# Dropping zero products from the set-up of a fused convolution and feed-forward kernel, moving set-up work between engines and between matmuls, and its last store to ScalarE

## The chip, the cores and the metric

The kernel runs on one core of a Trainium2 chip. The metric is the device time of one execution in microseconds (us), the lower the better. A core has five engines: TensorE (PE in the profile: matmuls), VectorE (DVE), ScalarE (ACT), GpSimd (POOL) and SyncE (SP, which mostly issues DMA transfers).

## The reference

```python
# x: 8 x 4160 x 192, weight: 8 heads x 7 taps
w = softmax(weight)                                  # over the 7 taps
y[b, s, h, :] = sum_k w[h, k] * x_pad[b, s + k, h, :]      # causal convolution, 24 channels a head
y = y.reshape(33280, 192)
h = maximum(maximum(y @ w1, y @ w2), y @ w3)         # 192 x 768 each
out = h @ w_out                                      # 768 x 192, fp32 out
```

## The kernel before

The 33280 tokens are cut into 65 blocks of 512. For each block TensorE does the convolution as matmuls with a banded matrix (`band`), then the "first layer" `l1(t, j)` for six tiles j of 128 hidden units, then the second layer with `w_out`.

The kernel saves a third of the first layer with a rearrangement: max(y·w1, y·w2, y·w3) = max(relu(y·(w1−w3)), y·(w2−w3)) + y·w3. So the set-up has to compute the differences `wd` (w1−w3 in 64 partitions, w2−w3 in the other 64) and the product m = w3·w_out, so that out = h·w_out + y·m. For m it first transposes w3 on TensorE.

```python
def keep_warm(n, pool=psw, tag="w"):      # n products of zeros, to raise TensorE's clock
    ps = pool.tile([P, NBLK], FP32, tag=tag, name="idle")
    for _ in range(n):
        nc.tensor.matmul(ps[:], lhsT=idle[:, 0:P], rhs=idle[:], start=True, stop=True)

def make_wd(j0, j1):                      # the differences for tiles j0 .. j1-1
    f = slice(P * j0, P * j1)
    nc.vector.tensor_sub(out=wd[:, :, f], in0=ws[:, :, f], in1=w3s[:, :, f])

def make_m(i):                            # a part of m = w3 . w_out
    ps = psp.tile([P, D], FP32, tag="p", name=f"pm{i}")
    ...                                   # 6 or 12 matmuls of w3t and wo
    nc.vector.tensor_copy(out=m16[:, i, :], in_=ps[:])

def cross(t, cs=range(NC)):               # second copy of y in the other 64 partitions: VectorE
    ...
def cross_dma(t):                         # the same by two transfers inside SBUF
    yd = dense[t]
    nc.sync.dma_start(out=yd[HALF:P, 0:NC:2, :], in_=yd[0:HALF, 0:NC:2, :])
    nc.sync.dma_start(out=yd[0:HALF, 1, :], in_=yd[HALF:P, 1, :])

def l1(t, j):
    ...                                   # lp and lq: 3 + 3 matmuls into two PSUM tiles
    nc.scalar.activation(out=r[:, 0:N], in_=ps[0][:, 0:N], func=AF.Relu)
    nc.vector.tensor_max(out=hs[t][:, j, 0:N], in0=r[:, 0:N], in1=ps[1][:, 0:N])
```

The order in which the set-up is written is the order on each engine:

```python
    conv_dense(0, (nc.scalar.copy, nc.scalar.copy, nc.scalar.copy))   # first convolution
    keep_warm(4)
    cross(0, (0,))
    make_wd(1, 2)
    cross(0, (1, 2))
    l1(0, 0)
    ...
    conv_dense(1, (nc.scalar.copy, nc.scalar.copy, nc.scalar.copy))   # second convolution
    keep_warm(4)
    cross(1)
    make_wd(2, 3)
    l1(1, 0)
    ...                                   # tiles of blocks 0 and 1 with the rest of the set-up
    l1(0, 5)
    cast_dense(2, (nc.gpsimd.tensor_copy, nc.gpsimd.tensor_copy))
    conv_dense(2, (nc.scalar.copy, nc.vector.tensor_copy, nc.scalar.copy))   # third convolution
    ...
    cross_dma(2)
    ...
    make_m(0)
    make_m(1)
    l1(1, 4)                              # "the next first layer" below
```

The softmax here doesn't subtract the row's maximum and nothing guards it: scores larger than these inputs give would overflow.

## Time and profile before

Three runs gave 479.44, 480.50 and 480.67 us, median 480.5. The profiled execution took 479.41 us; its span on the core is 477.6 us.

| | busy us | share of span |
|---|---|---|
| TensorE | 470.7 | 99% |
| VectorE | 365.7 | 77% |
| ScalarE | 325.6 | 68% |
| GpSimd | 213.2 | 45% |

TensorE sets the time. The main loop gives it work without a gap, two blocks in about 13.95 us, and the change leaves the loop alone. What can be won lies in the first 31 us and in the last 4. This is TensorE's own timeline of before, with its start and busy time in us, the line, what it computes, the shape and the count, and in brackets how long it had stood still and for whom:

```profile
4.97 3.59 PE L215 MATMUL idle<-idle 128*128 128x512 f16 x8
8.49 1.90 PE L318 MATMUL D<-band,xz 112*32 112x103 f16 x60
10.33 1.04 PE L215 MATMUL idle<-idle 128*128 128x512 f16 x4
...
24.44 1.09 PE L318 MATMUL D<-band,xz 112*32 112x103 f16 x60
26.89 0.37 PE L374 MATMUL lp<-yd,wd 64*128 64x512 f16 x1
```

The eight zero products take 3.59 us, the four later ones 1.04: the first ran at half clock (0.43 us apart), the later at full clock (0.22 apart). L318 is a convolution. The first starts at 8.49, the third at 24.44, and the next first layer follows it by 2.45 us.

### The profile page before, as it was taken

How to read it: one execution, taken by the hardware profiler on the slowest of the kernel's cores; microseconds unless marked ns; L12 is line 12 of the kernel's file. 1: busy time of each engine (PE TensorE's matmuls, PEld its weight loads, DVE VectorE, ACT ScalarE, POOL GpSimd, SP SyncE). 2: the span in 40 equal slices, each digit the busy share in tenths (PEclk: the TensorE clock that was granted, in tenths of full speed). 3: DMA queues.
4: the chain of work that ended last, by engine and by line, in shares of the span. 5: the costliest groups of instructions: out<-in, count | busy, mean ns of one | idle time of the engine just before them, and what ended most of it. 6: DMA issues, size and time to landing. Idle time of an engine off the chain costs nothing.

```text
span 477.6 us, 21859 instructions
## 1 busy us (share of the span) xinstructions
PE 470.7 (99%) x9042; PEld 392.3 (82%) x9042; DVE 365.7 (77%) x610; ACT 325.6 (68%) x610; POOL 213.2 (45%) x347
## 2 busy tenths in 40 slices
PE   8999999999999999999999999999999999999995
PEld 4478888888888888888788888888888888888995
DVE  4767778778777877877777787877778787777774
ACT  4757666676666767666676766667667666766664
POOL 3636543553454355255445534534553454455200
PEclk9999999999999999999999999999999999999999
DMA  8775866666765666657577667656676765764423
GB/s 191 166 198 151 238 186 175 179 180 162 197 192 159 175 172 185 169 162 201 152 193 183 181 164 205 177 152 190 171 183 166 201 180 153 190 172 107 107 76 100
DMA packets 68481, 81.68 MB, mean 171 GB/s; under 512 B 9342, under 2 KB 57470, under 8 KB 68382
## 3 DMA queue, kind: packets, MB, share of 16 engines
q1 hardware_dynamic: 55438, 49.51, 41.6%
q0 software_dynamic: 12928, 30.78, 21.2%
q8 instruction: 71, 1.16, 1.1%
q14 instruction: 28, 0.23, 0.2%
q10 hardware_dynamic: 16, 0.00, 0.0%
HBM read 30.31 MB, written 25.56 MB: 117 GB/s over the span
## 4 chain that ended last, share of the span: by engine, by line
PE 97%; DVE 1%; issue 0%; ACT 0%
PE lp L374 32%; PE po L418 30%; PE lq L374 26%; PE G L299 7%; PE idle L215 2%; PE D L318 1%; DVE h L379 0%; PE band_cols L237 0%; DVE yd L334 0%; DVE yd L325 0%; DVE w3s L258 0%; ACT yd L324 0%; DVE wd L254 0%; DVE m L284 0%; DVE o L428 0%
## 5 line engine op out<-in xcount | busy, mean ns | idle before, releaser
L379 DVE TENSOR_TENSOR h<-r,lq 128x512 f16<-128x512 f16 x390 | 267.2, 685 | 100.0 <-ACT r L378 98.6
L378 ACT ACTIVATE r<-lp 128x512 f16<-128x512 f32 x390 | 232.8, 597 | 138.6 <-PE lp L374 91.2
L374 PE MATMUL lp<-yd,wd 64*128 64x512 f16 x1170 | 315.6, 376 | 0.1
L374 PE MATMUL lq<-yd,wd 64*128 64x512 f16 x1170 | 314.7, 375 | 0.8 <-DVE h L379 0.6
L418 PE MATMUL po<-wo,h 64*128 64x192 f16 x3120 | 230.2, 243 | 0.0
L418 PEld LDWEIGHTS <-h 64*128 64x128 f16 x3120 | 186.2, 94 | 25.8
L374 PEld LDWEIGHTS <-wd 64*128 64x128 f16 x2340 | 163.9, 93 | 24.1 <-issue 4.2
L444 POOL DMA_DIRECT2D out_dram<-o x64 | 51.2, 799 | 237.0 <-DVE o L428 221.7
L357 POOL DMA_DIRECT2D yd<-ys x183 | 92.7, 512 | 1.8 <-ACT ys L344 1.0
L418 PE MATMUL po<-m,yd 64*128 64x192 f16 x780 | 86.9, 243 | 0.0
L428 DVE TENSOR_TENSOR o<-a,po 128x384 f32<-128x384 f32 (+1 forms) x132 | 71.4, 542 | 1.0 <-ACT a L427 1.0
L427 ACT COPY a<-po 128x384 f32<-128x384 f32 (+1 forms) x132 | 61.7, 468 | 1.8 <-PE po L418 1.8
L418 PEld LDWEIGHTS <-yd 64*128 64x128 f16 x780 | 54.7, 94 | 8.1
L151 POOL CAST x<-xf 112x960 f16<-112x960 f32 x60 | 59.6, 995 | 2.5 <-DMA xf<-in_x_dram 2.4
L344 DVE CAST ys<-G 128x512 f16<-128x512 f32 x61 | 39.2, 683 | 0.0
L299 PEld LDWEIGHTS <-x 112*32 112x32 f16 x2400 | 28.6, 96 | 12.7 <-issue 12.3
L344 ACT CAST ys<-G 128x512 f16<-128x512 f32 x61 | 32.9, 588 | 1.3
L299 PE MATMUL G<-band,x 112*32 112x103 f16 (+1 forms) x2400 | 33.3, 209 | 0.0
L215 PE MATMUL idle<-idle 128*128 128x512 f16 x24 | 9.2, 527 | 1.2 <-DVE idle L210 1.2
L170 POOL CAST xz<-xf 112x240 f16<-112x240 f32 (+2 forms) x15 | 4.9, 375 | 7.7 <-DMA xf<-in_x_dram 7.3
L215 PEld LDWEIGHTS <-idle 128*128 128x128 f16 x24 | 2.6, 122 | 5.5 <-issue 3.8
L318 PEld LDWEIGHTS <-xz 112*32 112x32 f16 x240 | 4.7, 107 | 2.5 <-DVE wd L254 0.8
(48 smaller groups left out, 47.2 us busy)
## 6 DMA issues: line engine op xcount, KB each, us to landing
xf<-in_x_dram SPq DMA_DIRECT2D x57, 420.0 KB, 4.5
out_dram<-o POOLq DMA_DIRECT2D x62, 384.0 KB, 4.2
yd<-yd SPq DMA_DIRECT2D x61, 192.0 KB, 3.7
yd<-ys SPq DMA_DIRECT2D x61, 48.0 KB, 3.8
yd<-ys POOLq DMA_DIRECT2D x61, 48.0 KB, 3.5
xf<-in_x_dram SPq DMA_DIRECT2D x8, 252.0 KB, 4.3
yd<-ys POOLq DMA_DIRECT2D x61, 32.0 KB, 3.5
yd<-ys SPq DMA_DIRECT2D x61, 32.0 KB, 3.4
```

The costliest lines, as they stand in the source:

```text
L151: nc.gpsimd.tensor_copy(out=v[0:rl, q0:q1, :], in_=xf[0:rl, q0:q1, :])
L215: nc.tensor.matmul(ps[:], lhsT=idle[:, 0:P], rhs=idle[:], start=True, stop=True)
L299: nc.tensor.matmul(G[i][32 * g:32 * g + 32, lo:hi], lhsT=x16[0:rlen, cb:cb + 32], rhs=band[0:rlen, h, cc:cc + hi - lo], start=True, stop=T ...
L344: copy(out=slots[t][:, i, :], in_=convs[t][i][:])
L357: (nc.sync, nc.gpsimd)[n % 2].dma_start(out=yd[r0:r0 + rows, c, :], in_=slots[t][s0:s0 + rows, half, :])
L374: nc.tensor.matmul(ps[i][:, 0:N], lhsT=wd[row, c, P * j:P * (j + 1)], rhs=y[row, c, 0:N], start=(c == 0), stop=(c == NC - 1))
L378: nc.scalar.activation(out=r[:, 0:N], in_=ps[0][:, 0:N], func=AF.Relu)
L379: nc.vector.tensor_max(out=hs[t][:, j, 0:N], in0=r[:, 0:N], in1=ps[1][:, 0:N])
L418: nc.tensor.matmul(ps[b0, i][:, s % 2, :], lhsT=a, rhs=b, start=first, stop=last)
L427: nc.scalar.copy(out=a[:, ss, :], in_=ps[s0, 0][:, ss, :])
L428: nc.vector.tensor_add(out=outs[t][:, s0:s + 1, :], in0=a[:, ss, :], in1=ps[s0, 1][:, ss, :])
L444: qs[0].dma_start(out=bass.AP(tensor=out.tensor, offset=r * D, ap=[[D, n], [step * D, s1 - s0], [1, D]]), in_=ob[p0:p0 + n, s0:s1, :])
```

## The change

The intent is to shorten the set-up and the end. Six zero products go. Three subtractions of 384 columns (128 in each of three parts) go from VectorE to GpSimd, the last two joined into one of 768, since VectorE's work stands ahead of work that TensorE waits for. The transposes and the first product of m are placed between other first layers, its copies go to ScalarE. The last of the final stores is issued by ScalarE, because SyncE is late with it. The core of the diff:

```diff
-    keep_warm(8, psp, "p")
+    keep_warm(5, psp, "p")
 ...
-    def make_wd(j0, j1):
+    def make_wd(j0, j1, eng=nc.vector):
 ...
-        nc.vector.tensor_copy(out=m16[:, i, :], in_=ps[:])
+        nc.scalar.copy(out=m16[:, i, :], in_=ps[:])
 ...
-                    store(t, s - (s == 1), s + 1, (nc.sync,))
+                    store(t, s - (s == 1), s + 1, (nc.scalar if s == 3 else nc.sync,))
 ...
-    make_wd(1, 2)
+    make_wd(1, 2, nc.gpsimd)
 ...
-    keep_warm(4)
+    keep_warm(3)
     cross(1)
 ...
     cast_w3(2)
-    keep_warm(1)
+    transpose_w3(1)
+    make_wd(4, 6, nc.gpsimd)
     l1(0, 3)
-    make_wd(4, 5)
-    transpose_w3(1)
+    transpose_w3(2)
     l1(1, 2)
-    make_wd(5, 6)
-    keep_warm(1)
     l1(1, 3)
-    transpose_w3(2)
     l1(0, 4)
     nc.gpsimd.tensor_copy(out=wo[:], in_=wos[:])
+    make_m(0)
     l1(0, 5)
 ...
-    make_m(0)
     make_m(1)
```

More of the change, by code (lines that the diff above doesn't have):

```diff
@@ L250 @@
     m16 = const.tile([P, 2, D], FP16)
-    def make_wd(j0, j1):
+    def make_wd(j0, j1, eng=nc.vector):
         f = slice(P * j0, P * j1)
-        nc.vector.tensor_sub(out=wd[:, :, f], in0=ws[:, :, f], in1=w3s[:, :, f])
+        eng.tensor_sub(out=wd[:, :, f], in0=ws[:, :, f], in1=w3s[:, :, f])
     def copy_w3(copy, part):
@@ L306, in conv, with conv_dense @@
         xin.pop(t)
-    def conv_dense(t, copies, pools=((psw, "w"), (psw, "w"))):
+    def conv_dense(t, copies):
         yd = dense[t] = ydp.tile([P, NC, NBLK], FP16, tag="yd", name=f"yd_{t}")
         for n, slots_ in enumerate((range(4), range(4, 6))):
-            ps = pools[n][0].tile([P, NBLK], FP32, tag=pools[n][1], name=f"D{n}_{t}")
+            ps = psw.tile([P, NBLK], FP32, tag="w", name=f"D{n}_{t}")
             for (q, b, row_lo, rlen, lo, hi, cc) in chunks_of[t]:
```

## The prediction

> **What bounds the kernel now.** I read the page first. Its busy line and its slices say where a change can pay:
>
> ```profile
> PE 470.7 (99%) x9042; PEld 392.3 (82%) x9042; DVE 365.7 (77%) x610; ACT 325.6 (68%) x610; POOL 213.2 (45%) x347
> PE   8999999999999999999999999999999999999995
> ```
>
> TensorE fills every slice but the first and the last (a slice is 477.6 / 40 = 11.9 us). The change touches neither the 63 blocks of the main loop nor their matmuls; it edits the set-up, which the timeline shows from 0 to about 31 us, and the last store. So its whole worth is idle and filler time in those two ends. The stretch view gives TensorE 15.59 us busy of the first 17 and 13.74 of the next 14.5, but part of that is products of zeros (24 of them, 9.2 us busy), so I went on to the chain of waits of the set-up:
>
> ```profile
> 13.58 0.69 DVE w3s L258
> 14.30 0.69 DVE h L379
> 15.02 0.91 DVE yd L334
> 15.97 0.37 PE lq L374
> ...
> 22.50 0.55 DVE wd L254
> 23.06 0.61 DVE h L379
> ...
> 25.75 0.69 DVE yd L325
> 26.48 0.37 DVE m L284
> 26.89 0.37 PE lp L374
> ```
>
> The set-up hangs on VectorE three times: around 14 us (copy of w3, a maximum, the copy yd that lets the second block's first layer start), at 22.5 (a subtraction ahead of a maximum that frees a PSUM buffer), and at 26.5 (m is copied out before the next first layer gets its PSUM buffer). Then GpSimd's own timeline, which shows what transfers dictate:
>
> ```profile
> 11.03 0.97 POOL L170 CAST xz<-xf 112x240 f16<-112x240 f32 x3 [7.33 <-DMA xf<-in_x_dram]
> ...
> 14.07 0.82 POOL L258 COPY w3s<-w3s 64x768 f32<-64x768 f32 x1 [0.54 <-DMA w3s<-in_moe_w_dram]
> 14.95 0.82 POOL L262 CAST w3h<-w3s 64x768 f16<-64x768 f32 x1
> 18.74 1.14 POOL L491 CAST wo<-wos 128x1152 f16<-128x1152 f32 x1 [2.97 <-DMA wos<-in_moe_w_out_dram]
> 20.27 3.96 POOL L170 CAST xz<-xf 112x240 f16<-112x240 f32 x12 [0.39 <-DVE h L379]
> ```
>
> The DMA engines are 0.94 busy over the first 17 us. The third block of x was issued at 13.57 and took 6.5 us, so it landed at 20.07: that, not the named maximum, is what the 12 casts at 20.27 waited for. The first six make block 2's input; SyncE issues the next load, which waits for them, at 22.26. So block 2's convolution, at 24.44 now, cannot run through before about 22.3 whatever the change does: 2.1 us is the ceiling of the set-up's gain.
>
> At the other end the last addition ends at 473.59, but SyncE is late with its last stores:
>
> ```profile
> 472.56 1.42 SPq L444 DMA_DIRECT2D out_dram<-o  x1
> 474.08 0.41 SPq L444 DMA_DIRECT2D out_dram<-o  x1
> 474.54 0.45 SPq L444 DMA_DIRECT2D out_dram<-o  x1
> ```
>
> The last store is issued 474.54 - 473.59 = 0.95 us after its data is ready, because an earlier issue took 1.42 us.
>
> **What the Trainium skill says.** "TensorE: Matmul & The Clock Gate", Part 1: the array starts at half clock and reaches full clock after a window of about 3.4 us of sustained work, at a phase that varies between runs. The trace agrees: idle matmuls of 512 columns last 0.63 us before 8.5 us and 0.39 at 10.33, and the first convolution's matmuls 0.29 against 0.21 later, so full clock came at about 10.3 us.
> "GPSIMD Engine Reference", 3.1: an fp32 two-input elementwise operation of 2048 columns takes 4497 ns on GpSimd. Scaled, an estimate from that page: 384 columns 0.84 us, 768 columns 1.69 us. The trace of before has no such operation on GpSimd; VectorE needs 0.556 for 384.
> "SBUF - State Buffer", "Who interferes with whom": a VectorE copy in a two-port mode and a GpSimd instruction exclude each other for the whole instruction. The trace agrees:
>
> ```profile
> 15.02 0.90 DVE L334 COPY yd<-yd 64x512 f16<-64x512 f16 x1
> ...
> 15.95 0.29 DVE L334 COPY yd<-yd 64x512 f16<-64x512 f16 x1
> ```
>
> The first copy ran into GpSimd's cast of 14.95 to 15.77. The same section lets VectorE's two-input operations contend with GpSimd's reads; here the subtractions at 21.44 and 22.50 ran beside the casts in an unchanged 0.55, so I charge those nothing.
> "DMA: Bandwidth & Descriptors", "Issuing engines are not separate DMA queues": a second issuing engine saves issue time only. That is just what the last store lacks.
>
> **The change part by part.**
> 1. *Three fewer zero products before the first convolution.* They run cold, 0.427 apart ((3.59 - 0.61) / 7), so the convolution starts 3 x 0.427 = 1.28 us earlier, at 7.2; its band is copied by 6.83, so it can. But full clock should still come near 10.3: the convolution then ends at 9.05, and of the four zero products that follow three run cold (1.28 us) instead of warm (0.65). The first layer of block 0 starts at about 10.5 instead of 11.30: **0.8 us** earlier.
> 2. *Subtraction 1 to GpSimd.* 0.56 us leave VectorE at 10.52. GpSimd is idle from 3.7 to 11.03 and the weights are there at 7.40; with 0.84 us (estimate) it is done by 8.4. Free, but the first layer it feeds did not wait for it: 0.
> 3. *Second convolution.* Block 1's x lands at 11.03, GpSimd's casts end at 12.0, ScalarE's, behind the relu of block 0, at 12.65 instead of 13.49. It keeps the 0.8 us. Copies of yd start at about 14.2 instead of 15.02.
> 4. *Here I take something back.* GpSimd's copy and cast of 14.07 to 15.77 stay where the weight transfer puts them, and the new 768-column subtraction follows at once, to about 17.5. VectorE's copy of w3 (now at 12.7) meets GpSimd's casts of 12.0 to 13.5, and the three yd copies meet the rest. Unhindered, the gain here is 0.8; with one instruction lost to the lock it is 0; with the long subtraction ahead of the last yd copy it is -1. I weigh these 0.5, 0.35, 0.15 and get 0.4 - 0.15 = **0.25 us**. A convolution at full clock earlier in some executions could add up to 0.4.
> 5. *First layers from 18.3 to 24.4.* Six in 6.15 us, 1.03 apart. With two PSUM buffers a pair needs relu 0.6, maximum 0.69, drain 0.37 and semaphores, about 2.0, so 1.0 each is the floor. Two subtractions (2 x 0.55) and two zero products (0.2 each) go, but only some 0.35 us of waits with them (0.33 and 0.2 to 0.35 at the last three). The product placed before the last first layer takes a turn of its PSUM pool, so that layer waits for a newer relu: -0.2. Net **0.15 us**.
> 6. *m on ScalarE, one product moved.* After the convolution the next first layer starts 24.44 to 26.89 = 2.45 us later; it becomes 1.03 + 0.62 = 1.65, 0.8 us less. But block 2's first layer, at 31.02, waits for the second yd transfer (issued 26.96, 4.0 us, landed 30.96), which hangs on the convolution, not on m. TensorE now gets there 0.15 us early; it will get there 0.95 early and wait. Worth **0**.
> 7. *Last store on ScalarE.* Issue at about 473.65 instead of 474.54, 0.9 us earlier; but the store before it is still issued at 474.08, and the 384 KB of the last three leave between 474.5 and 475.9 in nearly full engines. I count **0.35 us**.
> Sum: 0.25 + 0.15 + 0 + 0.35 = 0.75 us from these, and 0.2 for the chance of early full clock: 0.95.
>
> **Rivals.** *The lock on SBUF becomes the wait* (part 4): for it, the 0.90 copy above; against it, with the 0.8 shift one of the copies may slip in before 14.07. It alone would give about +1 us over my sum, 480.5. *All gains add up*: then the ceiling of block 2's casts binds, 2.1 us, and the store gives 0.5: 477.9. *The clock falls back to half* because zero products left: against it, gaps between matmuls stay near 1 us, far below a window; it would cost 2 to 3 us, 482. *The moved products feed through*: if the 0.8 of part 6 counts, 478.7.
>
> **Range and chances.** The three runs of before are 479.44 to 480.67, and the profiled one is among the fast (479.41), so the median itself carries some 0.6 us of luck. 480.5 - 0.95 = 479.55; before's mean of 480.2 would give 479.25; I say 479.4, with 478.2 to 480.6 for eight in ten. Two per cent is 9.6 us, beyond everything in the set-up that could be won or lost: within 2% at 0.98.
>
> **What would show it.** In the changed profile: the first convolution at 7.2 and the first layer of block 0 at 10.5 (part 1 right); a GpSimd subtraction of about 0.84 and one of 1.7 us; yd copies of VectorE longer than 0.29 beside it (part 4); block 2's convolution between 22.3 and 24.4, not waiting for its casts; block 2's first layer waiting for its yd transfer (part 6); the last store issued by ScalarE before 474 less the shift, and landing less than 0.5 us sooner relative to the last addition (part 7). The prediction is wrong if the convolution of block 2 starts later than now, if matmuls after 11 us last 0.6 us, or if the main loop's pace of some 7 us a block changes.

## The result, and the profile after

The changed kernel took 477.46 us (median of 4 runs, 476.62 to 478.37); the kernel before 480.29 (4 runs, three of them those that the prediction started from). The ratio is 0.9944 with an interval of 0.9921 to 0.9967. The class, within 2%, was right; the time lies 0.7 us below the range that was predicted.

The two profiled executions differ by 477.6 − 474.8 = 2.8 us of span. The busy line of the changed kernel's page shows no more than that of before where that is:

```profile
PE 467.0 (98%) x9036; PEld 390.7 (82%) x9036; DVE 365.2 (77%) x605; ACT 326.3 (69%) x612; POOL 216.1 (46%) x349
```

TensorE's timeline of the changed kernel does:

```profile
4.94 1.25 PE L215 MATMUL idle<-idle 128*128 128x512 f16 x5
6.92 1.09 PE L318 MATMUL D<-band,xz 112*32 112x103 f16 x60 [0.72 <-ACT band L241]
...
17.95 0.39 PE L374 MATMUL lp<-yd,wd 64*128 64x512 f16 x1 [0.69 <-DVE wd L254]
...
23.52 1.09 PE L318 MATMUL D<-band,xz 112*32 112x103 f16 x60
24.54 0.69 PE L282 MATMUL pm<-wo,w3t 128*64 128x192 f16 x12
25.16 0.39 PE L374 MATMUL lp<-yd,wd 64*128 64x512 f16 x1
```

Read it beside the lines of before. The five zero products take 1.25 us, 0.215 apart: here full clock was there at 4.94 already, and the first convolution waited 0.72 us for its band. In before's execution it came only at about 10. That is a difference of phase between two executions, not of the kernels, as the experiments will show. In the middle stands a wait that before did not have, 0.69 us for a VectorE subtraction. The next first layer follows the third convolution by 25.16 − 23.52 = 1.64 us instead of 2.45.

Set on one line, the time between marks in the two profiles:

| | before | changed | gained |
|---|---|---|---|
| start to third convolution | 24.44 | 23.52 | 0.92 |
| third convolution to next first layer | 2.45 | 1.64 | 0.81 |
| from there to the end of the last addition | 446.70 | 446.45 | 0.25 |
| last addition to the end of the span | 4.01 | 3.19 | 0.82 |

The chain of waits of the changed kernel (start, duration, what; "issue" is time for which the profile shows no reason) answers the one in the prediction:

```profile
16.33 1.00 DVE wd L254
...
23.59 1.02 PE D L318 x55
24.61 0.61 PE pm L282 x12
```

The copy of m is gone from it: after the convolution, TensorE goes from product to layer. VectorE's subtraction is in it for 1.00 us. Why it takes so long, GpSimd's timeline and VectorE's show:

```profile
7.86 1.36 POOL L254 TENSOR_TENSOR wd<-ws,w3s 128x384 f16<-128x384 f32 x1 [4.16 <-DMA ws<-in_moe_w_dram]
...
15.64 1.84 POOL L254 TENSOR_TENSOR wd<-ws,w3s 128x768 f16<-128x768 f32 x1 [0.24 <-DMA ws<-in_moe_w_dram]
```

```profile
7.81 0.56 DVE L254 TENSOR_TENSOR wd<-ws,w3s 128x384 f16<-128x384 f32 x1 [1.26 <-DMA ws<-in_moe_w_dram]
...
14.70 1.12 DVE L254 TENSOR_TENSOR wd<-ws,w3s 128x384 f16<-128x384 f32 x1
16.33 1.56 DVE L254 TENSOR_TENSOR wd<-ws,w3s 128x384 f16<-128x384 f32 x1
```

At 7.8 both engines start a subtraction together: VectorE's ends after its usual 0.56, at 8.37, GpSimd's at 9.22, which is 0.85 after that. At 15.64 GpSimd is in the middle of its own when VectorE starts one at 16.33: this one takes 1.56 and ends at 17.89, after GpSimd's end at 17.48. They take turns.

Part 6 of the prediction rests on the second of the two transfers that copy block 2's y. TensorE's matmul that needs it and the list of transfers, in before:

```profile
31.02 0.37 PE L374 MATMUL lp<-yd,wd 64*128 64x512 f16 x1
yd<-yd SPq DMA_DIRECT2D x1, 64.0 KB, 4.0
```

and in the changed kernel:

```profile
29.16 0.38 PE L374 MATMUL lp<-yd,wd 64*128 64x512 f16 x1
yd<-yd SPq DMA_DIRECT2D x1, 64.0 KB, 2.7
```

In before it was issued at 26.96 and landed 4.0 us later, at 30.96, just ahead of its matmul. In the changed kernel it was issued at 26.04 and landed at about 28.7, 0.4 us before its matmul, which did not wait. From the third convolution to this matmul it is 5.64 us instead of 6.58.

The end of the changed kernel, from the timelines of VectorE and ScalarE in this order (ACTq and SPq are issues of transfers by ScalarE and SyncE):

```profile
471.26 0.35 DVE L428 TENSOR_TENSOR o<-a,po 128x192 f32<-128x192 f32 x1 [0.17 <-ACT a L427]
```

```profile
471.65 0.39 ACTq L444 DMA_DIRECT2D out_dram<-o  x1
```

The last store is issued 0.04 us after its data is ready, where before took 0.95. The store ahead of it, still on SyncE, took 0.42 us to issue here. In each of the other nineteen profiles one of SyncE's last stores took 0.79 to 1.52 us, so the 1.42 us of before is the rule and this profile the exception.

### The profile page after: what moved, and what is told of

It is laid out like the page before. It is cut to its first block, busy times and chain, and to the rows that moved or that the text cites. A ratio compares the mean times of both kernels' runs of the same rounds, so it can differ in the third digit from the quotient of the medians.

```text
span 474.8 us, 21845 instructions
## 1 busy us (share of the span) xinstructions
PE 467.0 (98%) x9036; PEld 390.7 (82%) x9036; DVE 365.2 (77%) x605; ACT 326.3 (69%) x612; POOL 216.1 (46%) x349
## 4 chain that ended last, share of the span: by engine, by line
PE 95%; DVE 1%; DMA 1%; ACT 1%; issue 1%; SPq 0%; DVEq 0%
PE lp L374 32%; PE po L418 30%; PE lq L374 26%; PE G L299 7%; DMA ws<-in_moe_w_dram 1%; PE D L318 1%; DVE wd L254 0%; DVE yd L334 0%; DVE h L379 0%; SPq L183 0%; ACT r L378 0%; SPq L135 0%; ACT xz L170 0%; PE pm L282 0%; PE pm L278 0%
## 5 line engine op out<-in xcount | busy, mean ns | idle before, releaser
L215 PE MATMUL idle<-idle 128*128 128x512 f16 x18 | 5.8, 464 | 1.2 <-DVE idle L210 1.2
L318 PE MATMUL D<-band,xz 112*32 112x103 f16 (+1 forms) x240 | 4.9, 209 | 0.8 <-ACT band L241 0.7
L254 POOL TENSOR_TENSOR wd<-ws,w3s 128x384 f16<-128x384 f32 (+1 forms) x2 | 3.2, 1603 | 4.4 <-DMA ws<-in_moe_w_dram 4.4
```

What stands on the lines that cost most here:

```text
L318: nc.tensor.matmul(ps[32 * g:32 * g + 32, lo:hi], lhsT=xz[t][v][0:rlen, q, 32 * s:32 * s + 32], rhs=band[0:rlen, h, cc:cc + hi - lo], star ...
```

## The experiments

The main theory is that of the prediction, corrected by the result: the gain is the sum of small ones, of the zero products, of m and of the store, and GpSimd's subtraction gives some of it back through the lock. Its rivals are that one part makes nearly all of the 2.8 us (the zero products through the clock, or m through the layer that it lets start sooner), and that a part of the 2.8 us is chance in the few runs. So each part was first done alone on the kernel before, and then undone alone in the changed kernel; only the new places of the transposes were not tried apart. Each set has runs of before on its own chip (the first two and the fourth on one, the third and the fifth on two others), so sets are best compared by ratio. All kernels gave right results.

### Each part alone on the kernel before (6 runs each, before's median 479.13 in these rounds)

`e1_store`, the last store alone:

```diff
-                    store(t, s - (s == 1), s + 1, (nc.sync,))
+                    store(t, s - (s == 1), s + 1, (nc.scalar if s == 3 else nc.sync,))
```

> The kernel before with only the last store moved to ScalarE. In the profiles of before and after the time from the end of the last addition to the end of the span is 4.01 and 3.19 us. Theory A (the queue): SyncE's own stores hold the last one up in every execution, so this run's end takes about 3.2 us and the kernel is 0.8 us faster. Theory B (a hiccup): the 1.42 us issue in the profile of before is chance (the same issue takes 0.37 us after), so SyncE is free in most executions and the store alone is worth 0 to 0.2 us. The set-up is that of before unedited, so it is also a second look at when full clock comes: if the phase is free, not at 10.3 us again.

Measured: 479.05 us, ratio 0.9987 (0.9964 to 1.0010). The last addition to the end took 3.57 us instead of before's 4.01. One of SyncE's stores took 1.47 us again, so theory B's reason, a hiccup of before's, is wrong, though its 0 to 0.2 us fits. The 0.8 us of theory A did not come at the end of the profile; the times alone exclude neither.

`e2_m`, m alone:

```diff
-        nc.vector.tensor_copy(out=m16[:, i, :], in_=ps[:])
+        nc.scalar.copy(out=m16[:, i, :], in_=ps[:])
 ...
+    make_m(0)
     l1(0, 5)
 ...
-    make_m(0)
     make_m(1)
```

> The kernel before with only the first product of m placed before the last first layer of block 0, and both copies of m on ScalarE. Prediction on record: the interval from block 2's convolution to the next first layer falls from 2.45 to 1.65 us, but block 2's own first layer keeps waiting for its yd transfer, so the time stays the same (0). Rival from the two profiles: that layer waited only 0.15 us, and the transfer also comes earlier or lands faster, so the 0.8 us are kept: interval from block 2's convolution to block 2's first layer down from 6.2 to about 5.5 us and the kernel 0.6 to 0.8 us faster.

Measured: 479.26, ratio 0.9995 (0.9970 to 1.0019). The third convolution to the next first layer is 1.64 us, as in the changed kernel; the time shows nothing of it.

`e3_zero`, six zero products fewer:

```diff
-    keep_warm(8, psp, "p")
+    keep_warm(5, psp, "p")
 ...
-    keep_warm(4)
+    keep_warm(3)
 ...
-    keep_warm(1)
 ...
-    keep_warm(1)
```

> The kernel before with six fewer products of zeros (8 to 5, 4 to 3, and the two single ones gone) and nothing put in their place. If the array is cold until some 10 us, as in the profile of before, the first convolution starts 1.28 us earlier (7.2 instead of 8.49). If full clock comes near 5 us, as in the profile of after, the three of the eight are worth nothing, since five or eight products then end before or about when the band is copied (6.9 us). Theory A (zero products matter): 0.5 to 1 us faster in the median. Theory B (they fill waiting time, the clock's phase decides): within 0.3 us, and the clock never falls back below full after it once came.

Measured: 478.91, ratio 0.9983 (0.9960 to 1.0006). TensorE's timeline of this kernel:

```profile
4.97 2.31 PE L215 MATMUL idle<-idle 128*128 128x512 f16 x5
7.21 1.90 PE L318 MATMUL D<-band,xz 112*32 112x103 f16 x60
9.05 1.53 PE L215 MATMUL idle<-idle 128*128 128x512 f16 x4
```

This is the late phase of the clock: the five products are cold, the convolution is at 7.21 and takes 1.90, and of the four products after it some are still cold. The prediction had described just this.

`e4_sub`, the subtractions alone:

```diff
-    make_wd(1, 2)
+    make_wd(1, 2, nc.gpsimd)
 ...
+    make_wd(4, 6, nc.gpsimd)
     l1(0, 3)
-    make_wd(4, 5)
 ...
-    make_wd(5, 6)
```

> The kernel before with only the subtractions of columns 1, 4 and 5 on GpSimd. Theory A (VectorE was the limit of the first layers): 0.3 to 0.6 us faster. Theory B (lock on SBUF): VectorE's copies and subtractions beside GpSimd's subtractions take 0.9 to 1.6 us instead of 0.3 and 0.56, as in the profile of after, and eat the gain: 0 to 1 us slower. GpSimd's subtractions should take 0.84 and 1.7 us alone, up to 1.4 and 1.9 with a wait.

Measured: 479.88, ratio 1.0007 (0.9980 to 1.0033).

No one of the four is told from nothing, and none is worth 2.8 us: each interval excludes a gain of more than 0.4%, 1.9 us. Added up, the four ratios give −0.13 − 0.05 − 0.17 + 0.07 = −0.28%, or 1.3 us. So the rivals by which one part makes nearly all of the 2.8 us fall, and chance has to be looked at. That one part, the zero products say, makes most of a smaller gain, is not excluded.

### Each part undone in the changed kernel (before's median 479.33)

The runs of before are the eleven of the first set and one more. The edits are those above reversed: `u1_store` has the last store on SyncE again, `u2_m` the product and its copies as before, `u3_zero` the six zero products back, `u4_sub` all subtractions on VectorE.

```diff
u1_store:
-                    store(t, s - (s == 1), s + 1, (nc.scalar if s == 3 else nc.sync,))
+                    store(t, s - (s == 1), s + 1, (nc.sync,))
u2_m:
-        nc.scalar.copy(out=m16[:, i, :], in_=ps[:])
+        nc.vector.tensor_copy(out=m16[:, i, :], in_=ps[:])
 ...                                        (and make_m(0) back in its old place)
u3_zero:
-    keep_warm(5, psp, "p")
+    keep_warm(8, psp, "p")
 ...                                        (and 4 for 3, and the two keep_warm(1) back)
u4_sub:
-    make_wd(1, 2, nc.gpsimd)
+    make_wd(1, 2)
-    make_wd(4, 6, nc.gpsimd)
 ...                                        (and make_wd(4, 5), make_wd(5, 6) back)
```

> The changed kernel with the last store back on SyncE. If the queue holds it up in every execution, the end takes 4.0 us from the last addition instead of 3.19 and the kernel loses 0.8 us against the changed one (ratio to before up by 0.0017). If the 1.42 us issue was a hiccup, the end takes 3.2 to 3.5 us and the loss is under 0.3 us. It is also another look at the changed set-up with another phase of the clock.

> The changed kernel with both products of m after block 2's convolution again and their copies on VectorE. From block 2's convolution to the next first layer 2.45 us instead of 1.65. If the 0.8 us go through to the end (rival), the kernel loses 0.6 to 0.9 us against the changed one; by the prediction on record, which let block 2's yd transfer take the gain back, it loses under 0.2 us.

> The changed kernel with all six products of zeros back. Theory A (they stood in the way): loses 0.5 to 1.3 us against the changed one, most in executions where the array is still cold at 7 us. Theory B (they only fill waiting time): loses under 0.3 us.

> The changed kernel with all subtractions back on VectorE. Lock theory: in the profile of after GpSimd's subtractions held back a yd copy (0.97 instead of 0.29 us), and two of VectorE's subtractions (1.12 and 1.56 instead of 0.56), the last with 0.69 us of waiting on TensorE; so undoing them gains 0.3 to 1.0 us against the changed kernel. Rival (VectorE's time is what counts): three subtractions of 0.56 us come back into VectorE's chain of maxima, and it loses 0.3 to 0.6 us.

| | median us | ratio to before | interval |
|---|---|---|---|
| u1_store | 478.10 | 0.9965 | 0.9941 to 0.9989 |
| u2_m | 478.94 | 0.9982 | 0.9959 to 1.0005 |
| u3_zero | 479.46 | 0.9999 | 0.9975 to 1.0023 |
| u4_sub | 478.61 | 0.9983 | 0.9958 to 1.0007 |

Without the store's move the kernel stays 0.35% faster than before; with the zero products back nothing is left of the gain. For `u4_sub` the lock theory expected 0.3 to 1.0 us less than the changed kernel; its 0.9983 shows nothing of that. The profile of `u3_zero`, taken of its slowest run, shows a loss that is not what was removed. This is TensorE's timeline and a line of VectorE's:

```profile
17.58 0.60 PE L374 MATMUL lp<-yd,wd 64*128 64x512 f16 x1 [1.15 <-DVE wd L254]
...
22.82 0.63 PE L374 MATMUL lp<-yd,wd 64*128 64x512 f16 x1
...
24.33 0.41 PE L374 MATMUL lp<-yd,wd 64*128 64x512 f16 x1
```

```profile
15.31 2.21 DVE L254 TENSOR_TENSOR wd<-ws,w3s 128x384 f16<-128x384 f32 x1
```

VectorE's subtraction, 0.56 us by itself, started beside GpSimd's long one and took 2.21. TensorE waited 1.15 us for it, and the matmuls that follow last 0.60 to 0.63 instead of 0.38 until 24.3: the clock went back to half for some 6.7 us. This execution's mean granted clock is 0.992 and it is the slowest of the six of `u3_zero` (481.01). So in one execution the lock did what could be put down to the zero products. That this kernel's other five runs (478.82 to 479.65) are also slower than all ten of the changed kernel on record and in `a1_again` (476.62 to 478.43) is not explained by it.

### The changed kernel again, and the subtractions in other places (before's median 479.38)

`a1_again` is the changed kernel unaltered, on another chip than the eight kernels above, though its expectation names theirs. `s1_late` is `u4_sub` with the first subtraction placed behind the VectorE copies of block 0. `s2_pool` is `s1_late` with the last two subtractions on GpSimd, one tile each and behind its cast of w_out. `g2_double` is the changed kernel with the long GpSimd subtraction done twice.

```diff
s1_late, against the changed kernel:
-    make_wd(1, 2, nc.gpsimd)
     cross(0, (1, 2))
+    make_wd(1, 2)
 ...                                        (and the last two subtractions on VectorE, as in u4_sub)
s2_pool, against s1_late:
+    nc.gpsimd.tensor_copy(out=wo[:], in_=wos[:])
+    make_wd(4, 5, nc.gpsimd)
+    make_wd(5, 6, nc.gpsimd)
     l1(0, 3)
-    make_wd(4, 5)
 ...
-    make_wd(5, 6)
 ...
-    nc.gpsimd.tensor_copy(out=wo[:], in_=wos[:])
g2_double, against the changed kernel:
     make_wd(4, 6, nc.gpsimd)
+    make_wd(4, 6, nc.gpsimd)
```

> The changed kernel as it is, on the chip of the eight ablations. If 0.9944 on record holds, 2.7 us faster than before; if its four runs flattered it, the local marks (0.8 us from the moved product, 0.3 from the store, up to 1 from the zero products in late-clock executions, -0.5 to -2 from the lock) make 1 to 2 us, a ratio of 0.996 to 0.998. The profile should show full clock either at once in the second group of zero products or at about 10.3 us, as all ten profiles so far did.

> The changed kernel with all subtractions on VectorE and that of column 1 behind the three yd copies of block 0, where nothing waits for it yet. Lock theory: no VectorE copy or subtraction of the first layers stretched by GpSimd's subtractions; block 1's convolution to block 2's convolution in about 11.7 us instead of 12.5 to 13.8, and 0.5 to 1.2 us faster than the changed kernel of the same rounds. Rival (VectorE's time): within 0.3 us of it or slower.

> As s1_late, but columns 4 and 5 stay on GpSimd, as two subtractions of 0.85 us behind the cast of w_out, at about 18.5 to 20.2 us, when VectorE has only maxima left. Lock theory with VectorE's time on top: the best of the four, 0.1 to 0.4 us faster than s1_late. Against it: block 2's casts on GpSimd start 0.8 us later, which costs nothing while its convolution starts after 22.3.

> The changed kernel with the subtraction of columns 4 and 5 done twice on GpSimd (same values). Lock theory: another 1.7 to 1.9 us in which VectorE's subtractions cannot start; block 1's convolution to block 2's convolution 1 to 2 us longer than in the changed kernel, the kernel 0.7 to 2 us slower. Rival (GpSimd's time is free until block 2's casts): within 0.3 us.

| | median us | ratio to before | interval |
|---|---|---|---|
| a1_again | 477.93 | 0.9964 | 0.9945 to 0.9982 |
| s1_late | 477.69 | 0.9961 | 0.9942 to 0.9979 |
| s2_pool | 479.92 | 1.0012 | 0.9989 to 1.0035 |
| g2_double | 479.27 | 1.0004 | 0.9982 to 1.0026 |

The unaltered kernel gains 0.36% here, not 0.56%. All subtractions on VectorE (`s1_late`) do as well as the changed kernel, where the lock theory expected 0.5 to 1.2 us more. A second long subtraction on GpSimd costs 479.27 − 477.93 = 1.34 us, with intervals that just meet at 0.9982, and subtractions on GpSimd late in the set-up cost 479.92 − 477.69 = 2.23, with intervals that are apart. So more work on GpSimd in the set-up, or work at a worse place, costs time; `s2_pool` was expected to be the best of the four and is the worst. But the profiles do not show the lock as the reason. The second to the third convolution takes 12.73 us in `g2_double`, against 12.51 in `a1_again`, and `s2_pool` has the earliest third convolution of all twenty profiles (22.64). Both lose their time after it. In `s2_pool` TensorE waited for a transfer and then, from about 31.6 to 34.9, ran at half clock, as its timeline shows:

```profile
30.23 0.39 PE L374 MATMUL lq<-yd,wd 64*128 64x512 f16 x1 [1.59 <-DMA yd<-yd]
...
33.87 0.63 PE L374 MATMUL lp<-yd,wd 64*128 64x512 f16 x1
```

That is a wait for block 2's second copy of y, of the kind that the prediction expected in the changed kernel; here it ended with the first of the two transfers (128 KB), which took 5.3 us instead of before's 2.4. Three of the six runs of `s2_pool` have a mean granted clock of 0.996. The chain of waits of `e1_store` has the second of them:

```profile
25.66 4.90 DMA yd<-yd
```

### Without that transfer (before's median 479.69)

To take this wait away, the two transfers of block 2 were replaced by VectorE copies, in the changed kernel (`a2_cross`), in before (`b2_cross`) and in `s1_late` (`s4_cross`). `s6_cast` is `s4_cross` with the last cast of w3 on ScalarE, to free GpSimd.

```diff
-    cross_dma(2)
+    cross(2)
s6_cast, in addition:
+    nc.scalar.copy(out=w3h[:, :, 2 * PW:3 * PW], in_=w3s[0:HALF, :, 2 * PW:3 * PW])
-    cast_w3(2)
```

> The changed kernel with block 2's two yd transfers replaced by VectorE copies (as blocks 0 and 1 have them). The prediction on record said that this transfer takes back what m's move gains; in the profiles so far block 2's first layer waited for it in some executions (0.3 to 2.2 us) and not in others. If the transfer binds in most executions of the changed kernel, this is 0.3 to 1 us faster than a1_again's 0.9964; if it seldom does, within 0.3 us. From the next first layer to block 2's own always 3.8 us, and its second matmul pair 0.2 after.

> The kernel before with the same replacement. In its profile block 2's first layer waited only 0.15 us for the transfer, in a second look (e1_store) 1.2 us. If the transfer was no limit before, within 0.3 us of before, so that the move of m was free to count in full; if it was, 0.3 to 1 us faster.

> s1_late (all subtractions on VectorE, the first behind the yd copies) with block 2's yd transfers replaced by VectorE copies. s1_late's convolution of block 2 came at 23.46 us, 0.6 before the changed kernel's, but its first layer then waited 1.5 us for the transfer. If that hid the gain, this is 0.5 to 1.2 us faster than both s1_late and the changed kernel, a ratio of 0.993 to 0.995; if not, 0.996.

> s4_cross with the last cast of w3 on ScalarE, so that GpSimd leaves the SBUF port to VectorE's yd copies of block 1 (they took 1.60 us in s1_late, 0.9 without a lock). By the lock, block 1's convolution to block 2's convolution 0.4 to 0.7 us shorter; by time 0.2 to 0.6 us faster than s4_cross, unless block 2's casts (about 22.3 us) already bind.

| | median us | ratio to before | interval |
|---|---|---|---|
| a2_cross | 478.96 | 0.9988 | 0.9973 to 1.0004 |
| b2_cross | 480.61 | 1.0016 | 0.9998 to 1.0034 |
| s4_cross | 476.86 | 0.9941 | 0.9922 to 0.9961 |
| s6_cast | 477.12 | 0.9950 | 0.9932 to 0.9967 |

Neither before nor the changed kernel became faster when the transfer was gone, and both came out slower than either case of their expectations allowed, though for `b2_cross` that is within the noise. In before VectorE's copies delay what follows the third convolution: in `b2_cross` the next first layer comes 3.29 us after it instead of 2.45. In `a2_cross` a later convolution also has a wait of 1.03 us that the profile puts down to nothing; that stayed open. `s4_cross`, which has no subtraction on GpSimd, was the fastest kernel so far, as expected; `s6_cast` added nothing to it.

### The two best beside each other (before's median 479.47)

`a3_third` is the changed kernel, `s4_again` is `s4_cross`, both unaltered, on a third chip.

> The changed kernel a third time, beside s4_again in the same rounds. From 0.9944 and 0.9964: a ratio to before of 0.995 to 0.997.

> s4_cross a second time, in the same rounds as the changed kernel. If s4_cross's 0.9941 was no luck, 0.993 to 0.996, and 0.3 to 1.2 us faster than a3_third. In the profile block 2's first layer should again wait for no transfer: 3.8 us from the next first layer to its own, 0.2 to its second pair.

Measured: `a3_third` 478.22, ratio 0.9985 (0.9966 to 1.0003); `s4_again` 477.40, ratio 0.9971 (0.9951 to 0.9991). The version without GpSimd subtractions and without the transfer is faster than before in both of its sets. In this one its median is 0.82 us under the changed kernel's, but the intervals overlap, so that it beats the changed kernel isn't settled.

The profiled execution of `a3_third` is the worst that the lock did to the unaltered changed kernel. TensorE's and VectorE's timelines:

```profile
16.69 0.37 PE L374 MATMUL lq<-yd,wd 64*128 64x512 f16 x1
...
19.14 0.61 PE L374 MATMUL lp<-yd,wd 64*128 64x512 f16 x1 [2.08 <-DVE wd L254]
```

```profile
16.12 2.96 DVE L254 TENSOR_TENSOR wd<-ws,w3s 128x384 f16<-128x384 f32 x1
```

GpSimd's last cast of w3 had started at 16.09, its long subtraction at 16.88, because the weight transfer had come late. VectorE's subtraction ended at 19.08, after both; TensorE waited 2.08 us and came out of it at half clock for about 3 us. In the first profile of the same kernel the subtraction took 1.56 and the wait was 0.69.

### What the profiles say together

Twenty profiled executions of seventeen kernels give the same marks, in us: the start of the second and of the third convolution, from the third to the next first layer, from there to the end of the last addition, and from that to the end of the span. The last four columns of a row sum up to its span. The clock is called early where the second group of zero products already runs 0.215 apart, so by 4.9 us, and late where it still runs 0.43 apart; full clock then came between about 8.4 and 10.8:

| | zero products in the second group | clock | 2nd conv. | 3rd conv. | to next layer | to last addition | end |
|---|---|---|---|---|---|---|---|
| before | 8 | late | 12.88 | 24.44 | 2.45 | 446.70 | 4.01 |
| changed | 5 | early | 11.01 | 23.52 | 1.64 | 446.45 | 3.19 |
| a1_again | 5 | late | 11.57 | 24.08 | 1.64 | 446.72 | 3.76 |
| a3_third | 5 | late | 11.60 | 25.88 | 1.64 | 446.54 | 3.64 |
| e1_store | 8 | early | 11.15 | 23.15 | 2.45 | 447.83 | 3.57 |
| e2_m | 8 | early | 11.23 | 24.20 | 1.64 | 447.08 | 3.98 |
| e3_zero | 5 | late | 11.91 | 23.37 | 2.45 | 446.50 | 3.78 |
| e4_sub | 8 | late | 13.29 | 26.02 | 2.45 | 446.83 | 3.60 |
| u1_store | 5 | early | 11.62 | 25.41 | 1.64 | 446.42 | 3.63 |
| u2_m | 5 | late | 12.19 | 23.86 | 2.46 | 447.10 | 3.68 |
| u3_zero | 8 | early | 10.98 | 27.10 | 1.64 | 446.81 | 3.65 |
| u4_sub | 5 | late | 11.90 | 23.57 | 1.64 | 446.43 | 3.56 |
| s1_late | 5 | late | 11.95 | 23.46 | 1.64 | 448.02 | 3.58 |
| s2_pool | 5 | early | 11.53 | 22.64 | 1.84 | 450.06 | 3.56 |
| g2_double | 5 | late | 11.46 | 24.19 | 1.64 | 448.00 | 3.47 |
| a2_cross | 5 | late | 11.80 | 23.82 | 1.65 | 447.74 | 3.69 |
| b2_cross | 8 | late | 13.33 | 24.11 | 3.29 | 446.52 | 3.78 |
| s4_cross | 5 | late | 12.26 | 23.80 | 1.65 | 446.48 | 3.57 |
| s6_cast | 5 | late | 11.88 | 23.07 | 1.64 | 446.91 | 3.68 |
| s4_again | 5 | late | 11.88 | 23.42 | 1.65 | 446.81 | 3.62 |

Three things can be read from it, with one profile a kernel as a caution. Among the executions with the late clock and all subtractions on VectorE, the third convolution starts at 24.44 and 24.11 with eight products (`before`, `b2_cross`) and at 23.07 to 23.80 with five (six profiles, mean 23.45), about 0.8 us sooner. With the clock late, the second to the third convolution takes 10.8 to 11.7 us where all subtractions are on VectorE (eight profiles), and 11.7 to 14.3 where the long one is on GpSimd (six). And the stretch to the last addition is 446.4 to 447.1 us but for five kernels: four that wait for block 2's transfer (447.83 to 450.06), and `a2_cross` with its unexplained wait.

## Why the prediction was right or wrong

The time, 477.46 us, is below the range of 478.2 to 480.6. Two things made the difference of 1.9 us to the predicted 479.4, and the first is not in the changed kernel.

**The start of the sum was too high.** The prediction subtracted 0.95 from 480.5 and conceded "some 0.6 us of luck". Over all 49 runs of the kernel before the mean is 479.53 and the median 479.44, the changed kernel's mean over 16 runs is 477.98. So the three runs of before were slow against the pool (by 1.0 us in their median, 0.7 in their mean), and the four of the changed kernel about half a us fast. This is the rival of chance, and it holds. Pooled, the change is worth 479.53 − 477.98 = 1.55 us; from the scatter of the runs (0.84 and 0.88 us), its interval is an estimated 1.0 to 2.1. The predicted gain, 0.95 or the 1.1 from 480.5 to 479.4, lies at its lower edge. The gain was therefore probably undersized too, by an estimated half a us; without the eight runs on record the pool gives 1.32 (0.8 to 1.9), which leaves that open.

**Part 6 is the step of the sum that failed in the recorded profile.** "Worth 0", because "TensorE now gets there 0.15 us early; it will get there 0.95 early and wait". The 0.8 us of it was sized right: the layer follows the third convolution by 1.64 in the changed kernel against 2.45. But the wait did not come in the recorded profile, and from the third convolution to the matmul that was to wait the whole 0.94 us was gained (6.58 to 5.64). The prediction took the transfer's 4.0 us as fixed. In the changed kernel it took 2.7, and over the kernels that have it 2.4 to 4.9. TensorE does not wait for it in any of the three profiles of the changed kernel, and waits 0.54 to 1.59 us in those of `e1_store`, `s1_late`, `s2_pool` and `g2_double`, where it took 4.1 us or more and the first transfer of the pair 4.3 to 5.3. So the rival "the moved products feed through" was right where the transfer was short. What it is worth on average isn't settled by times: alone 0.05% (`e2_m`), and undoing it leaves 0.9982 instead of 0.9964 (`u2_m` and `a1_again`, on two chips), with intervals of ±0.2%.

**Part 1, the zero products: right mechanism, one phase missing.** The prediction took full clock at 10.3 us for granted. The profiles show two phases. Where the clock comes late, the second convolution starts at 13.17 on average with eight products (3 profiles) and at 11.85 with five (11 profiles): 1.3 us, where 0.8 was predicted. The step before it came just as told in `e3_zero`: first convolution at 7.21, first layer at 10.51. Full clock then often came during or right after the first convolution, not at 10.3 (`a1_again` has its four products after it 0.22 apart from 8.92 on). Three profiles with eight are few, and not all of the 1.3 need be the products: in `b2_cross` the first layer starts at 10.38, sooner than in before, and its relu only at 12.17. Where it comes early, the band is what the convolution waits for, and removing the products is worth nothing: 11.12 with eight and 11.39 with five (3 profiles each). The pair of profiles has before in the late and the changed kernel in the early phase, which looks like 1.9 us of gain at the second convolution.

**Part 4, the lock: right in kind, too small in size in the profiles, not shown in the times.** The sum gave back 0.55 of the 0.8. The first-named rival was the lock as the wait, and it happened: from the second to the third convolution the two profiles of the changed kernel with the late clock take 12.51 and 14.28 us, against 11.56 in before and 11.5 to 11.7 in `u4_sub`, `s1_late` and `s4_cross`, where the subtractions are on VectorE and the clock is late too. The recorded profile takes 12.51 with the early clock, which is no evidence, since `e1_store` and `e2_m` take 12.00 and 12.97 with the early clock and all subtractions on VectorE. The times do not show it: neither `u4_sub` nor `s1_late` is faster than the changed kernel. One sentence was wrong: that VectorE's own subtractions can be charged nothing beside GpSimd. They had been seen beside small casts only. In the ten profiles with all subtractions on VectorE, those after the second convolution took 0.55 to 0.73 us each; in each of the nine with GpSimd's long subtraction in its early place, at least one took 1.08 to 2.96. The estimates of GpSimd's own durations held: 0.85 measured for 0.84 after the other had let go, 1.79 to 1.92 for 1.69 in the three profiles of the changed kernel (up to 2.22 in `a2_cross`).

**The rival that was dismissed, the clock falling back, exists.** "Gaps between matmuls stay near 1 us, far below a window": after waits of 1.15 (`u3_zero`) and 2.08 us (`a3_third`), amid other small ones, the matmuls ran at half clock, and in `s2_pool` after the wait of 1.59 us for the transfer. It is rare. Of the 54 runs of the nine with the last subtractions on GpSimd (`e4_sub`, `u1_store`, `u2_m`, `u3_zero`, `a1_again`, `a2_cross`, `a3_third`, `s2_pool`, `g2_double`) ten have a mean granted clock below 0.997; of the 54 runs of the nine without, one; of the 45 runs of before beside them, none. So the risk comes with the subtractions on GpSimd. The lock is shown as the reason in two profiles, `u3_zero` and `a3_third`; in `s2_pool`, which has three of the ten, the profiled wait was for a transfer; the other runs have no profile.

**Part 7, the store.** Predicted 0.35. The time from the last addition to the end is 3.80 on average in the six profiles with SyncE and 3.59 in the fourteen with ScalarE: 0.2 us. The reason given was right: with SyncE the last issue comes 0.41 to 1.04 us after its data in each of the six, and 0.03 to 0.04 with ScalarE. But little of that reaches the end. Of the 0.82 in the recorded pair, 0.2 is by which before's end is longer than the mean of the six, and 0.4 by which the changed kernel's 3.19 is shorter than the mean of the fourteen; it is the shortest of all, in the one profile without a slow issue on SyncE. `u1_store` (0.9965) and `e1_store` (0.9987) agree with so little.

**Parts 2, 3 and 5 and the ceiling.** The first subtraction on GpSimd was not as free as told: it ended at 9.22, not at 8.4, since VectorE held the port, and VectorE's copy of y after it took 0.97 where 0.29 is its free time. Parts 3 and 5 were not tested apart. The ceiling was not broken: in none of the twenty profiles does the third convolution start before 22.6. But it was not as fixed as told, since in the changed profile the first six of GpSimd's casts ran from 19.41 to 21.06, and only in `s2_pool`, whose casts begin at 21.23, were they about as late as the convolution. The main loop kept its pace.

What stays open: how the 1.55 us divide among the parts in time, as every interval is about as wide as a part; what the transposes' new places did; why undoing the subtractions (`u4_sub`) gained nothing; why a transfer of one size takes 2.4 in one kernel and 4.9 in another; and whether `s4_cross` beats the changed kernel.

## What to carry to other kernels

When a change is worth a few tenths of a per cent, first measure the spread of the kernel you start from: here the median of three runs was 1 us off the mean of 49, as much as the predicted gain itself. Don't read a gain from one pair of profiles, since the clock's phase, an end that was the shortest of twenty and a short transfer were part of the 2.8 us, where the pool of runs has 1.5. And before you hand VectorE's work to GpSimd to relieve it, look at what VectorE will run beside it: a subtraction that was 0.56 us became 1.1 to 3.0, and in two of nine such profiles TensorE lost its clock over the wait.

## What the Trainium skill lacked or had wrong

- "TensorE: Matmul & The Clock Gate", Part 1, has the clock go back to half after at least one idle window of about 3.4 us. Here it went back after full waits of 1.15 us (`u3_zero`), 2.08 us (`a3_third`) and 1.59 us (`s2_pool`), the first two in a stretch with shorter waits around them; matmuls then took 0.56 to 0.63 us instead of 0.38, for some 6.7, 3 and 3 us. The page has the run-variable phase of the first rise, and the runs agree: the changed kernel had full clock by 4.9 us in one profile and only by 8.9 in two.
- "SBUF - State Buffer", "Who interferes with whom", has VectorE's two-input operations contend with GpSimd's reads, and this is right: 0.56 us became 1.08 to 2.96. It does not say how little that can be: beside twelve small casts the same subtraction took 0.55 to 0.73 (ten profiles; before, at 21.44 and 22.50, 0.55).
- "DMA: Bandwidth & Descriptors", "Issuing engines are not separate DMA queues": a second issuing engine saves issue time only. The runs agree, with 0.2 us. No page has the spread of one issue on SyncE, 0.37 to 1.52 us for the same kind of store, nor that of one transfer inside SBUF, 2.4 to 4.9 us for the same 64 KB.
